# Attention forward and backward with a gated MLP on one core: ScalarE in program order, another order of loads at a hand-over, and a lag of seven row tiles

## The chip, the cores and the metric

The kernel runs on one core of one Trainium2 chip. The metric is the device time of one execution in microseconds (us). A ratio is the mean time of one kernel's fast runs over that of the other's of the same rounds, so it is not quite the ratio of the medians that are quoted. In the experiments the recorded ratios leave out the first, profiled run of each kernel, while the means that I quote in us keep it, so the two can differ by up to 2.5 us. In the profile lines PE is TensorE and PEld its weight loads, DVE is VectorE, ACT ScalarE, POOL GpSimd and SP SyncE; SPq is SyncE issuing transfers, and L958 is line 958 of the kernel. The granted clock is the share of TensorE's full clock that it was given, and the DMA share is the mean busy share of the 16 DMA engines.

## The reference

One layer, forward and backward. The layer is `out = x + attention(xn) * silu(mlp(xn))` with `xn = layernorm(x)`, 2048 rows of 576, 32 heads of 128 over a key and value cache of 2048, and a gated MLP of 4608. The outputs are `out` and the gradients of all inputs but one.

```python
def _A_ref(x, k_cache, v_cache, wq, wo):                 # H, Dh = 32, 128
    q = (x @ wq).reshape(B, Sq, H, Dh).transpose(0, 2, 1, 3)
    p = softmax(einsum("bhqd,bhkd->bhqk", q, k_cache) * Dh ** -0.5)
    o = einsum("bhqk,bhkd->bhqd", p, v_cache)
    return o.transpose(0, 2, 1, 3).reshape(B, Sq, H * Dh) @ wo
def _B_ref(x, w_gate, w_up, w_down):
    return (sigmoid(x @ w_gate) * (x @ w_up)) @ w_down
# ... x + s * g; reference() returns it and the vjp of grad_out
```

## The kernel before

Two stages matter here. In attention each head goes through 16 row tiles twice: first scores and exponentials, then their gradient. Each row tile leaves a slab of 128 x 2048 that a DMA transposes (PT in the first half, dST in the second), and a matmul group takes the transposed slab `SKEW` row tiles later. That distance is the lag, and one row tile's turn in a half is a slot.

```python
SKEW = 6
...
wpt = pool("wpt", 8 if fast else 4)          # transposed slabs in flight
...
def transpose_slab(hs, qt, name):
    T = wpt.tile([P, NT, P], bf, name=name, tag="PT")
    nc.sync.dma_start_transpose(T[:], hs.slabs[qt][:])
...
put(b1 + qt + skew, NT * P // 2, lambda qt=qt: tail1(hd(), qt, 0))   # reads PT
put(b2 + qt + skew, NT * P // 2, lambda qt=qt: tail2(hd(), qt, 0))   # reads dST
```

After attention comes the output projection: 16 row tiles, each a sum over 32 heads of the transposed attention output (oT) times rows of wo. Three oT buffers exist, which reuse the memory of KQ, xnT and xn_all, so in the profile tile 0's load is `KQ<-on_d`, tile 1's `xnT<-on_d`, tile 2's `xn_all<-on_d`. The last rows of wo are written over Kn, Vn and dOn, which attention frees last; heads whose rows lie there are "late", the others "early".

```python
loads[0] = row_loads(0)                       # dsg, g2b, xb of row tile 0
for st in range(1, R0):                       # R0 = 3
    if st > 1:
        nc.gpsimd.tensor_copy(oTs[st][0:1, 0, 0:1], loads[0][st % 3][0:1, 0:1])
    load_oT(oTs[st], st)
for view, h0, n, dead in wo_parts:
    if dead in (1, 2, 3):
        load_wo_rows(view, h0, 0, n)
for st in range(1, R0):
    loads[st] = row_loads(st)
...
def close(st):
    if st + R0 < NT:
        load_oT(oTs[st % 3], st + R0)
        loads[st + R0] = row_loads(st + R0)
    ...
for st in range(R0 - 1):
    mm(st, h_early)
for st in range(NT):
    mm(st, h_late if st in accs_of else h_early + h_late)
    close(st)
    if st == 0 and R0 > 1:
        mm(R0 - 1, h_early)
```

The copy of one element ahead of tile 2's load is not arithmetic: it reads what the first row loads bring and writes into the oT buffer, so it holds that load back until they have landed.

## Time and profile before

| | before |
|---|---|
| time | 4933.09 us, median of 3 (4931.61 to 4936.69) |
| TensorE busy, span | 4835.4 of 4929.9 us |
| one head of attention | 94.63 us, 32 heads |
| attention, projection, late stages | up to 3531.0, 143.4 and 1255.5 us |
| all waits of TensorE for transposed slabs | 13.1 us |
| waits in the hand-over to the projection | 6.8 us |

TensorE is the bound. The whole of its idle time is 4929.9 - 4835.4 = 94.5 us, of which the waits that the profile lists make up some 41; the rest lies before its first matmul and in gaps too short to list. The lines that carry this stand in the prediction.

### The profile page before, as it was taken

The page shows a single profiled execution, that of the slowest core. Times are in us where ns is not written, and L with a number is a line of the kernel's source. Part 1 is how long each engine was busy: PE and PEld are TensorE (multiplying, and loading weights), DVE is VectorE, ACT ScalarE, POOL GpSimd, SP SyncE. Part 2 cuts the span into 40 slices and gives each one's busy share as a digit, 9 for nine tenths or more (in the row PEclk, how much of TensorE's full clock was granted, in tenths as well). Part 3 has the DMA queues.
Part 4 walks back from the last instruction along what each step waited for, and adds up shares of the span by engine and source line. Part 5 has one row for each costly group of instructions (what it writes and reads, how often), then busy time and mean ns, then how long its engine had stood idle before and what let it go on. Part 6 is the DMA issues. An engine that isn't in the chain of part 4 may idle for free.

```text
span 4929.9 us, 100847 instructions
## 1 busy us (share of the span) xinstructions
PE 4835.4 (98%) x40273; PEld 2894.6 (59%) x41029; DVE 2802.5 (57%) x6554; ACT 2472.1 (50%) x4228; POOL 840.7 (17%) x1329
## 2 busy tenths in 40 slices
PE   9999999999999999999999999999899999999998
PEld 4445666666666666666666666666555555555554
DVE  4544666666666666656656666665434555554215
ACT  4431766766676676666667667667312111111111
POOL 3322111111111111111111111111221111111112
PEclk9999999999999999999999999999999999999999
DMA  7886999999999999999999999999999999998665
GB/s 260 274 201 170 225 227 231 215 227 230 227 232 224 230 227 227 233 221 233 223 224 228 232 226 223 232 229 224 225 221 234 230 232 225 226 224 213 187 173 153
DMA packets 3045845, 1097.11 MB, mean 223 GB/s; under 512 B 2949553, under 2 KB 2953778, under 8 KB 3045362
## 3 DMA queue, kind: packets, MB, share of 16 engines
q1 hardware_dynamic: 2946594, 771.07, 83.5%
q0 software_dynamic: 98160, 318.85, 20.5%
q8 instruction: 323, 5.29, 0.4%
q14 instruction: 160, 1.31, 0.1%
q10 hardware_dynamic: 608, 0.59, 0.0%
HBM read 175.31 MB, written 177.93 MB: 72 GB/s over the span
## 4 chain that ended last, share of the span: by engine, by line
PE 94%; DMA 2%; DVE 2%; issue 1%; ACT 1%; SPq 0%; POOL 0%; POOLq 0%; ACTq 0%; DVEq 0%
PE acc L683 18%; PE acc L744 18%; PE acc L998 13%; PE acc L1054 8%; PE dp L706 8%; PE sp L636 8%; PE acc L215 6%; PE u_ps L450 3%; PE dh L1111 3%; PE g_ps L448 3%; PE acc L533 3%; PE acc L958 2%; PE acct L145 1%; DMA dST<-Pq 1%; DVE Pq L709 1%
## 5 line engine op out<-in xcount | busy, mean ns | idle before, releaser
L654 ACT ACTIVATE Pq<-sp 128x1024 bf16<-128x1024 f32 x1024 | 1047.1, 1023 | 267.3 <-PE sp L636 224.3
L709 DVE SCALAR_TENSOR_TENSOR Pq<-dp,negdelta,Pq 128x1024 bf16<-128x1024 f32 x512 | 655.2, 1280 | 46.6 <-PE dp L706 45.2
L712 ACT ACTIVATE t<-dp,negdelta 128x1024 bf16<-128x1024 f32 x512 | 567.1, 1114 | 214.7 <-PE dp L706 165.3
L683 PEld LDWEIGHTS <-dST 128*128 128x128 bf16 x8192 | 508.2, 98 | 152.1 <-DMA dST<-Pq 11.0
L706 PE MATMUL dp<-VT,dOT 128*128 128x512 bf16 x1919 | 581.6, 379 | 2.4
L683 PEld LDWEIGHTS <-PT 128*128 128x128 bf16 x8192 | 500.1, 98 | 130.9 <-DMA PT<-Pq 11.1
L636 PE MATMUL sp<-KQ 128*128 128x512 bf16 x1858 | 568.9, 380 | 5.2 <-issue 5.2
L683 PE MATMUL acc<-Kn,dST 128*128 128x128 bf16 x8192 | 557.1, 219 | 8.8 <-DMA dST<-Pq 6.9
L683 PE MATMUL acc<-Vn,PT 128*128 128x128 bf16 x8192 | 542.1, 219 | 8.5 <-DMA PT<-Pq 6.2
L744 PE MATMUL acc<-Pq,dOn 128*128 128x512 bf16 x1983 | 527.3, 379 | 10.0
L713 DVE TENSOR_TENSOR Pq<-t,Pq 128x1024 bf16<-128x1024 bf16 x512 | 354.5, 692 | 316.7 <-ACT t L712 306.9
L744 PE MATMUL acc<-Pq,Qn 128*128 128x512 bf16 x2013 | 524.3, 380 | 4.9
L724 ACT ACTIVATE dq_n<-acc,rsc 128x128 bf16<-128x128 f32 x512 | 187.5, 366 | 333.7 <-PE acc L683 312.0
L1154 DVE TENSOR_TENSOR dxn<-acc,dxn 128x576 f32<-128x576 f32 x272 | 206.1, 758 | 247.8 <-PE acc L1054 247.8
L744 PEld LDWEIGHTS <-Qn 128*128 128x128 bf16 x2048 | 200.4, 98 | 240.9 <-issue 1.6
L744 PEld LDWEIGHTS <-dOn 128*128 128x128 bf16 x2048 | 198.8, 98 | 233.8
L1116 ACT ACTIVATE ndh<-dh 128x512 bf16<-128x512 f32 x144 | 86.0, 597 | 452.8 <-DVE du_blk L1114 449.0
L636 PEld LDWEIGHTS <-KQ 128*128 128x128 bf16 x2048 | 179.3, 98 | 127.7 <-issue 7.2
L641 DVE TENSOR_REDUCE rs_all<-rsp 128x1 f32<-128x2 f32 x512 | 78.5, 153 | 306.5 <-ACT Pq L654 295.0
L706 PEld LDWEIGHTS <-dOT 128*128 128x128 bf16 x2048 | 178.8, 98 | 124.4 <-issue 11.9
L677 POOL DMA_DIRECT2D on_d<-o_n x128 | 97.1, 759 | 778.8 <-DVE junk L695 447.8
L677 POOL DMA_DIRECT2D dq_d<-dq_n x128 | 97.9, 765 | 719.7 <-ACT dq_n L724 679.8
(208 smaller groups left out, 6794.4 us busy)
## 6 DMA issues: line engine op xcount, KB each, us to landing
out_dram<-kvn POOLq DMA_DIRECT2D x64, 512.0 KB, 4.7
ah<-a_d POOLq DMA_DIRECT2D x18, 1024.0 KB, 9.2
ah<-h_d POOLq DMA_DIRECT2D x18, 1024.0 KB, 12.1
h_d<-h_row POOLq DMA_DIRECT2D x64, 256.0 KB, 3.5
a_d<-a_row POOLq DMA_DIRECT2D x64, 256.0 KB, 3.8
x_all<-in_A_k_cache_dram SPq DMA_DIRECT2D x64, 256.0 KB, 3.8
on_d<-o_n POOLq DMA_DIRECT2D x128, 128.0 KB, 4.4
kvT_d<-KQ POOLq DMA_DIRECT2D x32, 512.0 KB, 5.3
```

What stands on the lines that cost most here:

```text
L215: nc.tensor.matmul(av[:, :CH], lhsT=w[:, i, :], rhs=srcT[:, i, cs], start=(i == 0), stop=(i == DT - 1))
L636: nc.tensor.matmul(sp[:, c * CH:(c + 1) * CH], lhsT=hs.QT[:, qt * P:(qt + 1) * P], rhs=hs.KT[:, hf * HW_ + c * CH: hf * HW_ + (c + 1) * CH ...
L654: nc.scalar.activation(Pq[:, hsl], sp[:], AF.Exp, scale=SCALE, accum_out=hs.rsp[:, hf:hf + 1])
L683: nc.tensor.matmul(hs.acc[:, 0, :], lhsT=T[:, kt, :], rhs=rhs[:, kt, :], start=(kt == 0), stop=(kt == NT - 1))
L706: nc.tensor.matmul(dp[:, c * CH:(c + 1) * CH], lhsT=hs.dOT[:, qt * P:(qt + 1) * P], rhs=hs.VT[:, hf * HW_ + c * CH: hf * HW_ + (c + 1) * C ...
L709: nc.vector.scalar_tensor_tensor(Pq[:, hsl], dp[:], hs.negdelta[:, qt:qt + 1], Pq[:, hsl], op0=ALU.add, op1=ALU.mult)
L712: nc.scalar.activation(t[:], dp[:], AF.Identity, bias=hs.negdelta[:, qt:qt + 1], scale=1.0)
L713: nc.vector.tensor_tensor(Pq[:, hsl], t[:], Pq[:, hsl], op=ALU.mult)
L744: nc.tensor.matmul(self.acc, lhsT=self.nat[:, qt, :], rhs=self.slabs[qt][:, cs], start=(qt == self.lo), stop=(qt == self.hi - 1))
L998: nc.tensor.matmul(acc[:, n0:n0 + nn], lhsT=lhs[:, st, cols], rhs=rhs[:, st, n0:n0 + nn], start=(st == 0), stop=(st == NT - 1))
L1054: nc.tensor.matmul(acc[:, n0:n0 + nn], lhsT=lT, rhs=w[:, n0:n0 + nn], start=(k == 0), stop=(k == len(terms) - 1))
L1154: nc.vector.tensor_tensor(dxn[:, st, :], acc[:, :D], dxn[:, st, :], op=ALU.add)
```

## The change

It has three parts. The lag goes from six to seven, with a ninth buffer for transposed slabs (paid for by smaller pools), so that a slab has one slot more to land. At the hand-over, wo's last rows are loaded ahead of the row loads, the rows that are freed last are loaded and summed last, and the holding copy is gone. In the late stages ScalarE keeps program order; before, a scheduler chose its order.

```diff
-    SKEW = 6
+    SKEW = 7
-            wpt = pool("wpt", 8 if fast else 4)
+            wpt = pool("wpt", 9 if fast else 4)
 ... (stat 8 -> 4 buffers, rs_all replaced by a small tile, junk in one buffer: room for the ninth slab)
-            tc.manual_schedule(engines={EngineType.SP, EngineType.Pool, EngineType.DVE, EngineType.PE}):
+            tc.manual_schedule():
-            h_late = [... for _, h0, n, dead in wo_parts if dead in (1, 2, 3) ...]
+            h_late = [... for _, h0, n, dead in sorted(wo_parts, key=lambda w: w[3] == 1) if dead in (1, 2, 3) ...]
-            loads[0] = row_loads(0)
             for st in range(1, R0):
-                if st > 1:
-                    nc.gpsimd.tensor_copy(oTs[st][0:1, 0, 0:1], loads[0][st % 3][0:1, 0:1])
                 load_oT(oTs[st], st)
-            for view, h0, n, dead in wo_parts:
+            for view, h0, n, dead in sorted(wo_parts, key=lambda w: w[3] == 1):
                 if dead in (1, 2, 3):
                     load_wo_rows(view, h0, 0, n)
+            loads[0] = row_loads(0)
```

More of the change, by code (lines that the diff above doesn't have):

```diff
@@ L598, in attention @@
             wsneg = None if fast else pool("wsneg", 3)
-            wpt = pool("wpt", 8 if fast else 4)
+            wpt = pool("wpt", 9 if fast else 4)
             wt, stg = pool("wt", 2), pool("stg", 2)
-            stat, hstat = pool("stat", 8), pool("hstat", 2)
+            stat, hstat = pool("stat", 4), pool("hstat", 2)
             ps_big = pool("ps_big", 2, space=PSUM)
@@ L610, in attention @@
             acc_box[0] = acc_alloc
-            warm = stat.tile([P, 1], f32, name="warm")
+            warm = stat.tile([P, 1], f32, name="rs")
             nc.scalar.activation(warm[:], eps_t[:], AF.Exp)
@@ L618, in start_head @@
                 hs = heads_pre[h] if h == 0 else new_head(h)
-                hs.rs_all = hstat.tile([P, NT], f32, name="rs_all")
                 hs.rinv_all = hstat.tile([P, NT], f32, name="rinv_all")
@@ L640, in row_sums @@
             def row_sums(hs, qt):
-                nc.vector.tensor_reduce(hs.rs_all[:, qt:qt + 1], hs.rsp[:], axis=AX.X, op=ALU.add)
-                nc.vector.reciprocal(hs.rinv_all[:, qt:qt + 1], hs.rs_all[:, qt:qt + 1])
+                rs = stat.tile([P, 1], f32, name="rs")
+                nc.vector.tensor_reduce(rs[:], hs.rsp[:], axis=AX.X, op=ALU.add)
+                nc.vector.reciprocal(hs.rinv_all[:, qt:qt + 1], rs[:])
                 hs.PT[qt] = transpose_slab(hs, qt, "PT")
@@ L693, in tail1 @@
                 alt.scaled(hs.o_n[:, qt % G4, :], op_[:, 0, :], hs.rinv_all[:, qt:qt + 1], eng=("s" if qt >= NT - skew else "v"))
-                junk = wt.tile([P, P], f32, name="junk")
+                junk = wt.tile([P, P], f32, name="junk", bufs=1)
                 nc.vector.scalar_tensor_tensor(junk[:], op_[:, 0, :], -1.0, hs.dOn[:, qt, :], op0=ALU.mult, op1=ALU.mult,
@@ L882 @@
     with late("pc") as pc, late("pcf") as pcf, \
-            tc.manual_schedule(engines={mybir.EngineType.SP, mybir.EngineType.Pool, mybir.EngineType.DVE, mybir.EngineType.PE}):
+            tc.manual_schedule():
         xn_all = pc.tile([P, NT, D], bf, name="xn_all")
@@ L925 @@
             h_early = [h0 + k for _, h0, n, dead in wo_parts if dead not in (1, 2, 3) for k in range(n)]
-            h_late = [h0 + k for _, h0, n, dead in wo_parts if dead in (1, 2, 3) for k in range(n)]
+            h_late = [h0 + k for _, h0, n, dead in sorted(wo_parts, key=lambda w: w[3] == 1) if dead in (1, 2, 3) for k in range(n)]
             oTs.append(oT_view(xn_all[:].rearrange("p t d -> p (t d)"), 0))
```

## The prediction

> **What bounds the kernel now.** I read the busy digits first, then the waits of TensorE by stretch, then the timeline where it waits. The busy view says that TensorE is the bound everywhere:
>
> ```profile
> PE   9999999999999999999999999999899999999998
> PEclk9999999999999999999999999999999999999999
> ...
> PE 94%; DMA 2%; DVE 2%; issue 1%; ACT 1%; SPq 0%; POOL 0%; POOLq 0%; ACTq 0%; DVEq 0%
> ```
>
> In the chain that ended last PE has 94%. A change of buffers and order can win only the rest, and only where PE stands still. So I looked at where it does. The waits of PE in attention (484 to 3535 us) and after it:
>
> ```profile
> PE acc L683 <- DMA dST<-Pq: 6.9, 6, 3.3
> PE acc L683 <- DMA PT<-Pq: 6.2, 5, 1.7
> PE sp L636 <- issue: 5.2, 2, 2.7
> ```
>
> ```profile
> PE acc L958 <- DMA Kn<-in_A_wo_dram: 2.8, 1, 2.8
> PE acc L958 <- DMA Vn<-in_A_wo_dram: 2.8, 1, 2.8
> PE acc L1054 <- DMA dqbT<-ah: 1.6, 1, 1.6
> PE acc L958 <- DMA xn_all<-on_d: 1.2, 1, 1.2
> ```
>
> (waiter, what ended the wait, us in total, times, longest.) The first two lines are the transposed slabs that come too late, all in all 11 waits in 1024 slabs. The second fence is the output projection, which waits for rows of wo (written over Kn and Vn) and for the third row tile's transposed attention output (in xn_all). The measured total is small: some 20 us of 4930.
>
> How regular attention is: every 64th weight load of line 636 starts a head. The distance is 94.63 us in 25 of the 31 gaps or within 0.01 of it; it is 98.78, 95.30, 95.25 and 96.26 after heads 5, 13, 22 and 23, and 89.61 in the first head, which has no head before it to finish. So a head without a wait costs 94.63, and the excess is 4.15 + 0.67 + 0.62 + 1.63 = **7.1 us**.
>
> The clock shows that a wait costs more than itself (window, PE, PEld, DVE, ACT, POOL busy, granted clock, DMA share, GB/s):
>
> ```profile
> 3440.00:3510.00 70.00, 66.28 (x605) 42.28 (x615) 49.22 (x134) 45.85 (x76) 13.52 (x26) 1.00 1.17 232
> 3510.00:3535.00 25.00, 21.46 (x184) 13.72 (x186) 7.24 (x10) 6.25 (x12) 2.41 (x4) 0.86 1.13 238
> 3535.00:3560.00 25.00, 17.97 (x112) 8.50 (x114) 2.98 (x4) 0.70 (x2) 10.78 (x20) 0.75 0.88 213
> 3560.00:3690.00 130.00, 127.95 (x1075) 71.22 (x1094) 44.54 (x76) 22.18 (x52) 33.05 (x60) 0.99 0.88 215
> ```
>
> The timeline of PE in the hand-over from attention to the projection:
>
> ```profile
> 3547.80 1.60 PE L958 MATMUL acc<-Kn,KQ 128*128 128x512 bf16 x6 [2.77 <-DMA Kn<-in_A_wo_dram]
> 3552.16 1.60 PE L958 MATMUL acc<-Vn,KQ 128*128 128x512 bf16 x6 [2.76 <-DMA Vn<-in_A_wo_dram]
> 3553.57 1.63 PE L958 MATMUL acc<-dOn,KQ 128*128 128x512 bf16 x6
> 3556.37 3.04 PE L958 MATMUL acc<-dsT,xn_all 128*128 128x512 bf16 x12 [1.16 <-DMA xn_all<-on_d]
> ...
> 3564.41 0.90 PE L958 MATMUL acc<-Kn,xnT 128*128 128x512 bf16 x6
> ```
>
> Six matmuls take 1.60 after the wait and 0.90 when the clock is back.
>
> **What the Trainium skill says.** "TensorE: Matmul & The Clock Gate", Part 1: The HAM clock gate: the array falls to half its clock after an idle window of about 3.4 us and needs about as long a busy one to return. The trace agrees: after the wait of 3.26 us at 3514.54 sixteen matmuls took 1.89 us, two slots earlier 1.06, and full pace is back at 3520.4. The same page, Architectural detail: ScalarE works its queue strictly in order. The trace agrees: a copy whose PSUM was complete at about 4914.8 ran at 4918.52, right behind an activation that waited for VectorE. So an order of ScalarE can matter. "DMA: Bandwidth & Descriptors", Issuing engines are not separate DMA queues: all queues share the same 16 engines. The trace agrees: the DMA share is 1.17 while slabs, wo rows and stores run together, and the transpose into xn_all, issued at 3540.43 beside three loads of wo rows, was awaited until 3556.37. The same page, Rules for kernel authors, says to issue early and wait late; that is what each part of this change does.
>
> **The change part by part.**
>
> *Lag seven, nine buffers.* No matmul is added or removed. The transposed slab of a row tile is now read one slot later. A slot is 94.63 / 32 = 2.96 us on average, so each slab has that much more time to land; the ninth buffer keeps the same spare (eight for six, nine for seven). The waits in heads 5, 13, 22 and 23 are 0.3 to 2.2 us long (weight loads included), below 2.96, so all should go: -7.1. Has ScalarE or VectorE room for the seventh tail in the other half of a head? In slots 5 and 6 of the score half PE needs 2.62 us. ScalarE starts one exp 1.14 after another there, and a dq copy adds 0.31: 2 x 1.14 + 0.31 = 2.59. It just fits, and the next slot has no dq copy. In the dp half VectorE had 0.52 idle in every second slot (5.24 us), with the tail's work in it. So I take 94.63 as unchanged. In the first head one tail of 16 x 55.8 ns = 0.89 moves into the second half and ramp slots 6 and 8 become about 0.2 longer: -0.7, including two short waits there.
>
> *The end of attention.* Here the lag helps little. The queue of transposes:
>
> ```profile
> 3481.24 23.32 SPq L630 DMA_TRANSPOSE dST<-Pq  x8
> 3504.67 4.80 SPq L584 DMA_TRANSPOSE KQ<-on_d  x1
> 3509.55 18.30 SPq L630 DMA_TRANSPOSE dST<-Pq  x8
> 3527.96 4.64 SPq L584 DMA_TRANSPOSE xnT<-on_d  x1
> ```
>
> It issues without a pause, some 10 us behind the slabs, because the last head also loads wo rows. The last dST landed at about 3530.2 and PE took it at 3530.54: at the end the transposes set the time, not the lag. Waits of PE before that (1.7, 0.4, 1.0, 3.3 and 3 of slow clock) turn into waits a little later. After the last slab PE has one slot's units instead of two: 6 matmuls of 0.215 us instead of 10, -0.9, and 0.2 nearer the landing: -1.1.
>
> *wo rows first, no copy that holds back xn_all.* The three loads of wo rows were issued at 3540.72, 5.9 us after the last kvT store (3534.85), behind three row loads and a GpSimd copy that waited for them. They now follow the store at once, Vn and dOn first and Kn, which is free last, last; the transpose into xn_all no longer waits for that copy (3540.22) and can go right after the one into xnT, at about 3532.7. Without any wait PE would go from the early heads of tile 1, which end at 3544.9, through the late heads of tile 0 (3 x 0.735 = 2.2) and the early ones of tile 2 (5.6) to 3552.7, where the trace has 3564.41: the whole hand-over is worth 11.7 at most. Will the loads land in time? kvT store 0.5 MB, wo rows 1.33 MB and xn_all 0.5 MB are 2.3 MB; the same stretch moved 3.65 MB in 18.7 us, 195 GB/s. That is 12 us from 3533.4, thus 3545.4, where PE wants the first rows at 3543.8 and the last at 3545.3. I leave 2 us of waits and 1.7 of slow clock: 11.7 - 3.7 = -8.0.
>
> *Program order on ScalarE.* The instruction order of the two kernels differs in the late stages by three places only: one ndh ahead of three copies in the first block, and two activations of the last rows ahead of a dwo copy. The two waits of PE on ndh are 0.8 us in all, and VectorE sets them. At the end a copy comes later and may hold a PSUM tile 0.9 us, but the last rows go at VectorE's pace of 4.36 us each and PE is not behind them. I take -0.2.
>
> Sum: -7.1 - 0.7 - 1.1 - 8.0 - 0.2 = **-17.1**, from 4933.1 to **4916.0 us**, 0.35% faster.
>
> **The rivals.** (1) *The lag shifts ScalarE or VectorE onto the path.* Slots 5 and 6 leave ScalarE 0.03 us; if slot 6 stalls PE by 0.3 in each of 31 heads, that is +9, and the result is 4925. For it: dp of the sixth slot came 0.06 us after VectorE had freed its PSUM. Against it: 25 heads equal to 0.01 us, so there is slack that doesn't show. (2) *The loads move the wait, not the end.* All share the DMA engines; if wo rows, the kvT store and xn_all together land no sooner than at 3550, the hand-over gives 4 instead of 9: 4920. For it: xn_all alone took almost 16 us. (3) *The waits in attention are chance*, other heads in each run (times range over 5 us); then one slot more takes them all, also those of slower runs, and the last slabs come sooner as well: 4908.
>
> **Range and chances.** The two big terms are 7.1 (certain to 3) and 9.1 (certain to 4); rival 1 can cost 9, rival 3 bring 8. I take 4906 to 4926. Two per cent are 98 us, and all that PE waits for anywhere, slow clock included, is below 60: faster by over 2% has 1%, within 2% has 98.5%, slower has 0.5%.
>
> **What would show it.** Right: heads of 94.63 with no excess after 5, 13, 22, 23; hardly a wait of line 683 in the middle of attention, but one of some 3 us still in the last slots; wo loads straight after the kvT store; the third tile begun some 10 us sooner after the last head's start; the last 100 us unchanged. Wrong: heads longer than 94.63 with waits of sp or dp for ScalarE or VectorE; a hand-over as long as before; no wait left at the end of attention.

Five slips in that text, none of which moves the result. 26 of the 31 gaps between heads are 94.63, not 25. The waits in the two fences add up to some 27 us, not 20. The sixteen matmuls that took 1.06 us stood one slot earlier, not two. TensorE's whole idle time, with the gaps too short to list, is 94.5 us, not below 60; it still stays below the 98 us that two per cent would need. And not each part of the change issues a transfer earlier: program order on ScalarE does not.

## The result, and the profile after

The changed kernel took 4933.99 us (median of 4, 4930.88 to 4944.1) against 4934.89 us of the kernel before in the same rounds: ratio 1.0002, 95% interval 0.9984 to 1.0019. The predicted 4916 us and the range of 4906 to 4926 were missed: the class, within two per cent, was right, but nothing of the 17 us came.

The profiled run was the slowest of the four (4944.1 us), so its waits are somewhat more than usual. The same lines of its page as shown of before, the busy digits and the chain that ended last:

```profile
PE   8999999999999999999999999999899999999998
...
PE 94%; DMA 2%; issue 2%; DVE 1%; SPq 1%; ACT 0%; POOL 0%; POOLq 0%; ACTq 0%; DVEq 0%
```

TensorE is as much the bound as before. The waits of TensorE in attention, and then after it (waiter, what ended the wait, us in total, times, longest):

```profile
PE acc L683 <- DMA PT<-Pq: 10.0, 10, 2.1
PE acc L683 <- DMA dST<-Pq: 8.2, 6, 2.8
```

```profile
PE acc L956 <- DMA KQ<-on_d: 9.6, 1, 9.6
PE acc L1052 <- ACT dqT L40: 6.4, 1, 6.4
...
PE acc L996 <- ACT dqT L40: 0.7, 1, 0.7
...
PE acc L956 <- DMA Kn<-in_A_wo_dram: 0.4, 1, 0.4
PE acc L956 <- DMA Vn<-in_A_wo_dram: 0.3, 1, 0.3
```

Three things are to be seen. The slabs are waited for longer than before (18.2 against 13.1 us), in spite of the larger lag. The waits for wo's rows are nearly gone (0.7 against 5.6 us), as intended. And a wait of 9.6 us has come that was not there: for tile 3's transposed output. The timeline of TensorE around it, and below it tile 3's line and its load in the kernel before, where there is no wait:

```profile
3549.01 0.90 PE L956 MATMUL acc<-Vn,KQ 128*128 128x512 bf16 x6 [0.25 <-DMA Vn<-in_A_wo_dram]
...
3552.04 4.33 PE L956 MATMUL acc<-dsT,xn_all 128*128 128x512 bf16 x34
...
3557.68 0.90 PE L956 MATMUL acc<-Vn,xnT 128*128 128x512 bf16 x6
...
3572.36 5.78 PE L956 MATMUL acc<-dsT,KQ 128*128 128x512 bf16 x34 [9.55 <-DMA KQ<-on_d]
```

```profile
3555.23 4.83 SPq L584 DMA_TRANSPOSE KQ<-on_d  x1
3569.38 4.33 PE L958 MATMUL acc<-dsT,KQ 128*128 128x512 bf16 x33
```

The projection's first matmul is at 3537.32 here, against 3533.59 before. Tile 1's late heads begin at 3557.68, thus 20.4 us after that; before it was 3564.41 - 3533.59 = 30.8. That gain of over 10 us is real, and it is given back at tile 3. The queue of transposing loads shows what tile 3 waited for:

```profile
3537.61 5.04 SPq L584 DMA_TRANSPOSE xn_all<-on_d  x1
3552.24 11.33 SPq L584 DMA_TRANSPOSE KQ<-on_d  x1
```

Tile 3's load can only be issued when tile 0 has released its buffer, at 3552.24. The issue took 11.33 us instead of some 5, and TensorE could start on the data at 3572.36. The stretches of that time (window, its length, busy time of PE, PEld, DVE, ACT and POOL, granted clock, DMA share, GB/s); the first two are the end of attention and the hand-over, the last three a closer look:

```profile
3510.00:3537.00 27.00, 21.09 (x213) 13.34 (x212) 7.74 (x9) 7.59 (x15) 1.61 (x3) 1.00 1.12 232
3537.00:3572.00 35.00, 25.05 (x205) 12.94 (x202) 8.61 (x13) 3.08 (x8) 11.78 (x21) 0.90 1.13 200
3549.50:3553.00 3.50, 2.99 (x24) 1.49 (x23) 0.05 (x1) 0.70 (x2) 2.27 (x5) 1.00 1.03 366
3557.00:3568.00 11.00, 5.81 (x54) 3.14 (x52) 4.82 (x8) 2.38 (x6) 0.06 (x1) 0.87 1.20 106
3571.50:3574.50 3.00, 2.14 (x9) 0.93 (x10) 0.00 (x0) 0.00 (x0) 2.13 (x4) 0.50 1.22 250
```

The last number of a line is the one to look at. While wo's rows and row loads alone are moved, 366 GB/s flow. While transposing loads alone are moved, it is 250, and 276 to 300 once the first half microsecond of that window is past. While both are in flight, from 3557 to 3568, it is 106, though the DMA engines count as busy all the time (share 1.20). So the row loads and tile 3's load, issued together, slow each other here. This is not a fixed rate of such a mix: in the kernel before, 2.06 MB of plain and 0.61 MB of transposing loads went at 268 GB/s together from 3546 to 3556 us, and the slabs, stores and wo rows at the end of attention at 232 from 3440 to 3510. Why this mix is so much slower is not known.

The wait of 6.4 us on dqT lies at 4582.74, where a transpose of dqT stood in the queue behind others. It appears in this profile only, of twenty, so I put it down to chance.

### The profile page after: what moved, and what is told of

Read it like the earlier page. It is cut to its first block, busy times and chain, and to the rows that moved or that the text cites. A ratio compares the mean times of both kernels' runs of the same rounds, so it can differ in the third digit from the quotient of the medians.

```text
span 4942.3 us, 101605 instructions
## 1 busy us (share of the span) xinstructions
PE 4871.7 (99%) x41029; PEld 2891.4 (59%) x41029; DVE 2789.9 (56%) x6522; ACT 2477.1 (50%) x4260; POOL 840.5 (17%) x1328
## 3 DMA queue, kind: packets, MB, share of 16 engines
q0 software_dynamic: 98160, 318.85, 20.8%
## 4 chain that ended last, share of the span: by engine, by line
PE 94%; DMA 2%; issue 2%; DVE 1%; SPq 1%; ACT 0%; POOL 0%; POOLq 0%; ACTq 0%; DVEq 0%
PE acc L683 18%; PE acc L744 17%; PE acc L996 13%; PE sp L635 9%; PE dp L706 8%; PE acc L1052 8%; PE acc L215 6%; PE u_ps L450 3%; PE g_ps L448 3%; PE dh L1109 3%; PE acc L533 3%; PE acc L956 2%; PE acct L145 1%; DVE Pq L709 1%; DMA PT<-Pq 1%
## 5 line engine op out<-in xcount | busy, mean ns | idle before, releaser
L635 PE MATMUL sp<-KQ 128*128 128x512 bf16 x2048 | 609.8, 380 | 5.4 <-issue 5.4
L706 PE MATMUL dp<-VT,dOT 128*128 128x512 bf16 x2048 | 608.8, 379 | 2.2
L641 DVE TENSOR_REDUCE rs<-rsp 128x1 f32<-128x2 f32 x512 | 78.7, 154 | 369.1 <-ACT Pq L654 362.1
```

The lines of the kernel that those rows point to most:

```text
L635: nc.tensor.matmul(sp[:, c * CH:(c + 1) * CH], lhsT=hs.QT[:, qt * P:(qt + 1) * P], rhs=hs.KT[:, hf * HW_ + c * CH: hf * HW_ + (c + 1) * CH ...
L706: nc.tensor.matmul(dp[:, c * CH:(c + 1) * CH], lhsT=hs.dOT[:, qt * P:(qt + 1) * P], rhs=hs.VT[:, hf * HW_ + c * CH: hf * HW_ + (c + 1) * C ...
```

## The experiments

Eighteen runs were made, some of them of the same kernel, in five groups; a group ran on one chip with its own runs of the kernel before. Stage lengths below are measured alike in each trace: the first head is the distance of the first score weight loads of heads 0 and 1; the excess is the sum over heads 1 to 30 of what their length exceeds 94.62 us; the projection runs from its first weight load to its last; the late stages from there to the end. One thing has to be allowed for: the first weight load comes 2.58 us ahead of the projection's first matmul with a lag of six and 1.94 us with seven. So the projection of a kernel with a lag of seven looks 0.6 us shorter in these figures than it is beside one with six.

### Group 1: the change again, and its two large parts alone

The changed kernel, unaltered: 

> The changed kernel once more, unaltered. Theory A (a new wait took the place of the one removed): the profile again has a wait of PE on tile 3's transposed attention output (KQ<-on_d) at the hand-over, of 5 to 12 us, on every run, because that load can be issued only when tile 0 closes and now meets the row loads and has 7 us less time; the time stays within 0.2% of before. Theory B (a chance slow spell of the transposing loads in the one profile, at 800 to 1040 us and again at 3555 to 3572 us): the wait on KQ<-on_d is below 2 us here, the heads' waits sit in other heads or are gone, and the time falls towards 4920. The waits inside attention (10.3 us of excess in heads 4 and 5 of the first profile) should move to other heads under both theories; if they stay in heads 4 and 5 they are the change's own. The wait of 6.4 us on dqT in the last stage: if chance, it is gone or elsewhere here.

Median 4935.79 us of 5 (4927.23 to 4947.14), ratio 0.9995 (0.9982 to 1.0008). The wait on tile 3's load is there again, 9.65 us, and the projection took 147.5 us. So theory A holds for that wait. The excess in the heads, 17.9 us, sits once more in heads 3 to 5 (14 of it) but also in 19, 21 and 23. The wait of 6.4 us on dqT is gone.

The kernel before, for a second profile: 

> The kernel before, unaltered, only for a second profile. If the slow spells of the transposing loads are chance, the heads whose length exceeds 94.63 us are others than heads 5, 13, 22 and 23, with a total excess of 3 to 12 us; if they belong to the schedule, the same heads show them. The hand-over's gap (tile 1's late heads at 3564.41 in the first profile, some 143 us after head 31 begins) should be within 2 us of that in any case, since it is tied to the order of the loads.

One run, 4933.86 us. The excess is 5.1 us and lies in heads 4, 21, 24, 26 and 27, where the first profile had 5, 13, 22 and 23. Slow spells of the transposing loads thus fall elsewhere in each execution. Tile 1's late heads began 30.95 us after the projection did, against 30.82 in the first profile; counted from the start of head 31, as my expectation had it, they are 4.5 us later, since the end of attention itself varies.

The lag alone: 

> The kernel before with the lag of seven, the ninth buffer and the buffer cuts that pay for it, and nothing else of the change. My recorded sum gives this part -7.1 (waits inside attention) -0.7 (first head) -1.1 (end) = -9 us, so 4924 to 4926. The rival, that attention's waits are slow spells longer than the slack that one more slot of 2.96 us buys, gives -1 to -3 us, a ratio of 0.9995 or nearer to 1. Steady heads stay at 94.6 us under both. If ratio is above 1.0005, the lag costs something that neither names.

```diff
-    SKEW = 6
+    SKEW = 7        # with wpt 9, stat 4, rs in its own tile, junk in one buffer
```

Median 4927.16 us of 5 (4923.37 to 4938.07), ratio 0.9991 (0.9978 to 1.0004). The excess is 1.5 us, in one head, and the first head takes 88.2 us. On the mean it is 6.3 us faster than before: between the two expectations.

The reordered loads alone: 

> The kernel before with the reordering of the loads at the hand-over alone (wo's last rows ahead of the row loads, the last-freed rows summed last, no GpSimd copy ahead of tile 2's transposed load). My recorded term: -8 us (4925). Theory A above: tile 1's late heads begin 6 to 8 us earlier, but tile 3 begins no earlier than before, 148 to 150 us after head 31 begins, with a wait of 5 to 10 us on KQ<-on_d; the ratio is within 0.0005 of 1. Theory B: no such wait, ratio 0.998 to 0.9988.

```diff
 (the hand-over's part of the diff above, on the kernel before)
```

Median 4931.41 us of 6 (4923.08 to 4949.34), ratio 1.0001 (0.9985 to 1.0016). Here the projection took 136.8 us, 6.7 less than before, since the wait for tile 3 is only 3.2 us:

```profile
3559.78 3.83 PE L956 MATMUL acc<-dsT,KQ 128*128 128x512 bf16 x20 [3.22 <-DMA KQ<-on_d]
```

That is neither A nor B. It raised the question why the whole change has 9.6 us there, and led to theory C: the lag of seven makes it worse.

### Group 2: do the parts collide, and can the wait be taken away?

Lag and loads together, ScalarE as before: 

> The changed kernel with ScalarE's late order given back to the scheduler: lag seven and the reordered hand-over together. Theory C (the two parts collide: with the lag of seven the last transposes of attention and the projection's transposed loads are issued some 1.1 us later against the hand-over than in the run with the reordered hand-over alone, wo's rows take 10 to 12 us instead of 7 to 8, the row loads are pushed back, and tile 3's transposed load, issued then, takes 20 us instead of 14): the wait on KQ<-on_d is 8 to 11 us again, and the projection (first to last of its weight loads) takes 143 to 148 us. Theory D (ScalarE's order is what delays it): the wait is 3 us or less and the projection takes 136 to 138 us, as with the reordered hand-over alone. The wait of 0.7 us on dqT at line 996, seen in both profiles of the full change and in no other, should be gone in either case. Time within 0.1% of before under C, 0.998 under D.

```diff
-            tc.manual_schedule():
+            tc.manual_schedule(engines={EngineType.SP, EngineType.Pool, EngineType.DVE, EngineType.PE}):
```

Median 4931.64 us of 6 (4923.92 to 4945.54), ratio 0.9988 (0.9971 to 1.0006). The wait on tile 3 is 9.62 us and the projection 143.8: theory C, and not ScalarE's order. The time, 0.12% under before, lies between what C and D gave. The wait of 0.7 us on dqT is gone, as both expected.

A fourth oT buffer: 

> The changed kernel with a fourth buffer for the transposed attention output (in a slab that is free by then), so that tile 3's load is issued with those of tiles 1 and 2, ahead of the hand-over's row loads, and each later load when the tile that had its buffer closes. If tile 3's wait comes from its late issue, after tile 0's close: the wait on KQ<-on_d is gone (below 1 us) and the projection takes 133 to 137 us, 8 to 11 us less than in the full change; ratio 0.997 to 0.9985. Rival: the DMA engines are simply full in these 40 us, so the wait moves to wo's rows, to xn_all or to the tile after, and the projection still takes over 140 us.

```diff
+            oTs.append(oT_view(ah0[:].rearrange("p a t f -> p (a t f)"), 0))
+            oT_of = [0, 1, 2, 3] * 3 + [0, 1, 2, 0]
-            for st in range(1, R0):
+            for st in range(1, 4):
                 load_oT(oTs[st], st)
```

Median 4930.38 us of 6 (4921.15 to 4948.78), ratio 0.9985 (0.9965 to 1.0004). Tile 3 waits 2.1 us, tile 4 waits 3.2, wo's rows 0.8, and the projection takes 138.0 us: in part the first expectation, in part the rival. The wait moved, at over half its size.

Fewer row loads in flight: 

> The changed kernel with fewer row loads in flight at the hand-over: tile 1's rows are loaded when tile 0 closes, tiles 2 and 3's when tile 1 closes, and each later tile's two tiles ahead. Three oT buffers as before. If it is the row loads that slow tile 3's transposed load: it lands 12 to 15 us after its issue instead of 20, and the wait is 2 to 5 us; projection 136 to 140 us. If it is only the late issue, the landing still takes 18 to 20 us and the wait stays at 8 to 10 us. A loss is possible where a tile's rows come late for VectorE and hold back ScalarE's copies; it would show as waits of PE on s_sb at the projection.

```diff
             loads[0] = row_loads(0)
-            for st in range(1, R0):
-                loads[st] = row_loads(st)
 ...            (in close, after tile st's output is stored:)
+                for nx in ((1,) if st == 0 else (2, 3) if st == 1 else (st + 2,)):
+                    loads[nx] = row_loads(nx)
```

Median 4943.66 us of 6 (4927.6 to 4956.18), ratio 1.0009 (0.9989 to 1.0029). Tile 3 starts without any wait, 10.4 us after its load was issued at 3543.88, where the full change needs 20. So it is the row loads beside it that make this load slow. But the projection took 160.5 us, worse than I had allowed for: wo's rows were waited for 5.3 us, later tiles' loads 2.9 and 1.3, VectorE's late rows 2.3, and the last tile's load fell together with 2 MB that the next stage loads. The lines of that run, TensorE at tile 3 and the queue of transposes at the last tile:

```profile
3554.28 4.33 PE L954 MATMUL acc<-dsT,KQ 128*128 128x512 bf16 x33
```

```profile
3645.41 14.54 SPq L584 DMA_TRANSPOSE KQ<-on_d  x1
```

An issue of 14.54 us, and a wait of 9.5 us behind it: it looks like the same collision at another place. Why holding the rows brings these waits I did not follow up.

Program order alone: 

> The kernel before with program order on ScalarE in the late stages alone. My recorded term is -0.2 us. From the two profiles of the full change: one wait of 0.6 us on ndh goes, one of 0.7 us on dqT comes, so the late stages (end of the projection to end of the kernel) take 1255.0 to 1256.1 us, as in the kernel before (1255.5 and 1255.0). The 6.4 us wait on dqT of one of the two profiles was a late transpose: no such wait here.

```diff
-            tc.manual_schedule(engines={EngineType.SP, EngineType.Pool, EngineType.DVE, EngineType.PE}):
+            tc.manual_schedule():
```

One run, 4940.3 us, beside a mean of 4939.9 of the kernel before. The late stages took 1255.3 us, as expected; the wait of 0.7 us on dqT came, but the two on ndh stayed (0.8 us in all), so that it is the reordered loads that take one of them away.

### Group 3: repetition, the other direction, and the waits taken apart

Fourth buffer with held row loads: 

> The changed kernel with the fourth oT buffer of the run before, and the row loads of tiles 1 and 2 held until tile 0 closes, those of tiles 3 and 4 until tile 1 closes; from then on three ahead as ever. If late issue and contention with the row loads share tile 3's wait (the fourth buffer alone left 2.1 us on tile 3 and 3.2 us on tile 4; holding the rows alone made tile 3's load land in time), both waits are gone: projection 132 to 135 us and a ratio of 0.997 to 0.9985. Rival: wo's three row loads, which landed 9 to 17 us after issue in the runs so far, now end last, and the wait sits on them: projection 136 to 140 us.

```diff
 (the fourth buffer, and in close:)
-                    loads[st + R0] = row_loads(st + R0)
+                    if st > 1:
+                        loads[st + R0] = row_loads(st + R0)
 ...            (after tile st's output is stored:)
+                for nx in ((1, 2), (3, 4))[st] if st < 2 else ():
+                    loads[nx] = row_loads(nx)
```

Median 4929.72 us of 5 (4921.72 to 4933.6), ratio 0.9986 (0.9973 to 0.9999). Neither tile 3 nor tile 4 waits. In their place wo's first late rows are waited for 5.4 us, and the projection takes 138.4: the rival.

The reordered loads alone again: 

> The reordered hand-over alone once more, since its short projection (136.75 us, a wait of 3.2 us on tile 3) rests on one profile. Theory C (the lag of seven is what turns 3.2 into 9.6): 135 to 139 us and a wait of 2 to 5 us again. Rival (chance decides in each execution): a wait of over 8 us, projection 143 us or more.

Median 4937.8 us of 6 (4925.03 to 4940.94), ratio 1.0002 (0.9990 to 1.0013). Tile 3 waits 6.0 us, the projection takes 140.0. Just over my bounds, between the two readings: shorter than before, with a wait that varies.

A lag of five: 

> The kernel before with a lag of five row tiles instead of six, eight buffers as before: one step the other way. If the wait inside attention is a matter of slack, as my prediction's first term has it, one slot (2.96 us) less turns every place with under 3 us of slack in the trace of before into a wait: the heads' excess over 94.62 us rises from 5 to 11 us (four profiles at lag six) to 20 to 40, and the time by 0.3 to 0.7%. If a lag of one slot hardly matters, because the transposing queue is over 90% occupied and its backlogs outlast a slot, the excess stays at 5 to 14 us and the time within 0.2%. The first head, 89.6 to 90.1 us at lag six and 87.2 to 89.0 at seven, should take 91 to 92 us in either case.

```diff
-    SKEW = 6
+    SKEW = 5
```

Median 4959.13 us of 5 (4948.64 to 4962.24), ratio 1.0040 (1.0028 to 1.0053). The excess is 29.0 us and the first head takes 94.1. The waits of TensorE from head 1 to 30:

```profile
PE acc L683 <- DMA PT<-Pq: 15.6, 18, 2.1
PE acc L683 <- DMA dST<-Pq: 9.1, 13, 2.0
```

31 waits, where the kernel before has 6 in the same heads of its first profile. So slack is what counts; only the first head was worse than I had said.

The lag of seven alone again: 

> The lag of seven alone once more. Its first run stood at 0.9991 with an interval that holds 1, and its profile had 1.5 us of excess in the heads, against 0.1 to 17.9 in the five other profiles with a lag of seven. If the lag is worth my recorded -9 us, the ratio is 0.998 to 0.9985 and the excess again under 3 us; if it is worth only the first head's -1.8 us, the ratio is 0.9993 to 1.0 and the excess anything from 0 to 18. The projection takes 142 to 144 us with no wait on KQ<-on_d in either case.

Median 4932.03 us of 5 (4926.1 to 4935.91), ratio 0.9994 (0.9981 to 1.0006), excess 1.6 us, projection 143.2. The excess is as the first expectation had it, the ratio as the second.

### Group 4: why the whole shows less than its parts

The changed kernel a third time: 

> The changed kernel a third time. Summed from its parts alone (lag: -6.3 and -4.1 us on the mean of the runs; hand-over: -2.1 and -0.1; program order: none) it should gain some 5 us, but nine runs of it have shown +0.3. Theory E (chance: heads 4 to 6 fell into slow spells in both profiles): the mean of these five runs is 4 to 7 us under before, the excess in the heads 0 to 10 us. Theory F (something in the whole costs 5 us): the mean is within 2 us of before. The wait on KQ<-on_d of tile 3 is 8 to 11 us in both.

Median 4932.77 us of 6 (4927.23 to 4942.98), ratio 0.9995 (0.9977 to 1.0012); on the mean 1.7 us under before. Wait on tile 3: 10.3 us. Excess 8.8 us. This meets F, just, and not E, which wanted 4 us; with a spread of 16 us among the six runs the two can hardly be told apart.

Lag and loads again: 

> Lag seven and the reordered hand-over, ScalarE's late order left to the scheduler, once more (-6.9 us on the mean in its first rounds). Under E it stands where the full change stands in these rounds, within 3 us; under F, with the program order as the cost, it is 5 to 8 us faster than the full change, and its late stages are shorter by that much, which no profile so far shows. Wait on tile 3's load 8 to 11 us, projection 142 to 146 us.

Median 4930.3 us of 6 (4923.02 to 4937.94), ratio 0.9991 (0.9974 to 1.0007), 4.9 us under before and some 3 under the full change of the same rounds: between E and F. The late stages take 1255.3 us, no shorter. A miss in one point: tile 3 waited only 0.7 us, and the projection took 138.9. In this execution wo's rows came so late that they, not tile 3, were waited for:

```profile
3549.54 1.60 PE L956 MATMUL acc<-Vn,KQ 128*128 128x512 bf16 x6 [4.40 <-DMA Vn<-in_A_wo_dram]
...
3565.64 4.34 PE L956 MATMUL acc<-dsT,KQ 128*128 128x512 bf16 x33 [0.74 <-DMA KQ<-on_d]
```

When tile 3's load was issued, all but one of the twelve row loads of tiles 0 to 3 had been issued, and the last of them landed 3.9 us later; in the third run of the full change all but three, tile 3's own, and the last landed 18 us later. Tile 3's load was through within 12 us, there it took 20.8. It is the collision again, seen from its absence: where the two kinds of load overlap for only 3.9 us, the wait is nearly gone.

Program order alone, timed: 

> Program order on ScalarE alone, now timed. Under E: the mean within 2 us of before, late stages 1255 to 1256 us with one wait of 0.7 us on dqT more and one of 0.6 us on ndh fewer. Under F with the program order as the cost: 4 to 8 us slower than before.

Median 4940.2 us of 6 (4931.88 to 4949.55), ratio 1.0007 (0.9989 to 1.0025), on the mean 4.6 us slower. Late stages 1255.7 us, with the wait of 0.7 us on dqT. Excess 17.9 us. The time fits F, the late stages fit E.

Loads kept apart in time: 

> The changed kernel with a fourth oT buffer as before, but tile 3's transposed load held back until the last of wo's rows has landed (by a copy of one element that reads the one and writes the other), and the row loads of tiles 1 and 2 held until tile 0 closes. If the wait at the hand-over is contention between transposed loads and wo's rows in one direction and between row loads and transposed loads in the other, keeping the three apart takes both away: wo's rows land 9 to 12 us after the hand-over begins with a wait under 1 us, tile 3's load lands before 27 us, and the projection takes 132 to 135 us (143.5 before); ratio about 0.998. If wo's rows still land at 14 to 17 us, it was not tile 3's load that slowed them in the last run, and the projection takes 137 to 140 us.

```diff
+            nc.gpsimd.tensor_copy(oTs[3][0:1, 0, 0:1], wo_of[h_late[-1]][0:1, 0:1])
+            load_oT(oTs[3], 3)         # after loads[0] = row_loads(0); rows 1 to 4 held as above
```

Median 4932.15 us of 6 (4922.16 to 4938.47), ratio 0.9990 (0.9972 to 1.0007). Tile 3 doesn't wait, but wo's first late rows still land 15.8 us after the projection begins (a wait of 4.4), VectorE's late rows cost another 2.6, and the projection takes 142.3, more than either expectation. So it was not tile 3's load that slowed wo's rows in the run with the fourth buffer and held rows. What remains beside them is tile 2's transposing load, into xn_all, and the kvT store ahead of them.

That can be read across the runs with the reordered loads. wo's first late rows were always issued 2.08 us after the projection began. How late they landed goes, between groups, with when the load into xn_all was issued (both in us from the projection's first matmul):

| run | lag | xn_all issued | first late wo rows landed |
|---|---|---|---|
| loads alone, two runs | six | -1.28, -0.87 | 9.7, 9.0 |
| lag and loads; with fourth buffer | seven | -0.35, -0.48 | 10.7, 11.2 |
| full change, three runs | seven | 0.29, 0.31, 0.38 | 11.6, 14.3, 14.7 |
| lag and loads, second run | seven | 0.31 | 15.8 |
| held rows; fourth and held; timed; fourth and held without program order | seven | 0.22, 0.22, 0.21, 0.30 | 16.7, 16.8, 15.8, 15.6 |

In the last three lines the load is issued at nearly the same time and the rows land anywhere from 11.6 to 16.8, so the issue time is not the whole of it. With the holding copy in place, as in the kernel before, that load is issued at 6.8 to 7.0 whatever the lag, and the late rows at 7.1 and later. The copy did one thing that I had not seen: the kvT store, issued 1.25 us after the first matmul in every run, lands at 4.2 to 5.3 us in the eight profiles with the copy and at 7.7 to 12.0 in the twelve without it. No run keeps the copy and moves wo's rows alone.

### Group 5: a test of the pattern, and the version that is best

Program order alone, a third time: 

> Program order on ScalarE alone, a third time, as a test of a pattern seen only afterwards: the nine profiles with program order had 10.5 us of excess in the heads on average (0.1 to 17.9), the eight without it at lag six or seven 5.6 (1.5 to 12.0), though the instruction order in attention is the same. Chance: the mean of these runs within 3 us of before, excess anywhere from 2 to 12. A real cost of the whole program, by a way that I can't name: 4 to 6 us slower than before, excess 8 or more.

Median 4937.36 us of 6 (4924.91 to 4948.73), ratio 1.0003 (0.9988 to 1.0019), on the mean 2.7 us slower; excess 9.8 us. The time meets "chance", near its limit of 3 us, the excess both. The wait that program order brings, in this run:

```profile
PE acc L998 <- ACT dqT L40: 0.7, 1, 0.7
```

It is in all ten profiles with program order and in none without.

Fourth buffer, held rows and lag seven, ScalarE left to the scheduler: 

> The fourth oT buffer with held row loads and the lag of seven (0.9986 in its first rounds), with ScalarE's late order left to the scheduler: the candidate to beat both kernels. Chance: 0.9980 to 0.9992, as with program order. A real cost of program order: 0.9970 to 0.9980. The hand-over as in the run with program order: no wait on tile 3 or 4 above 1 us, one of 4 to 6 us on wo's first late rows, projection 137 to 139 us.

Median 4923.53 us of 6 (4921.27 to 4935.65), ratio 0.9981 (0.9968 to 0.9993), on the mean 9.1 us faster than before in the same rounds. The interval lies below 1, so this version beats the kernel before by some 0.2%, and its median lies 9 us or more under the changed kernel's of any group. It is the best of several tried, though, and has one set of rounds. The ratio meets "chance", at its edge. Its hand-over:

```profile
3545.57 1.60 PE L957 MATMUL acc<-Vn,KQ 128*128 128x512 bf16 x6 [4.21 <-DMA Vn<-in_A_wo_dram]
...
3559.80 4.33 PE L957 MATMUL acc<-dsT,ah 128*128 128x512 bf16 x33
```

Tile 3 (now in ah) starts without a wait, one wait of 4.2 us on wo's rows is left, and the projection takes 136.9 us.

### The stages side by side

| kernel | first head | excess, heads 1 to 30 | projection | late stages |
|---|---|---|---|---|
| before, 2 profiles | 89.6, 89.7 | 7.3, 5.1 | 143.4, 143.5 | 1255.5, 1255.0 |
| changed, 3 | 88.0, 89.0, 88.4 | 10.3, 17.9, 8.8 | 143.5, 147.5, 148.2 | 1263.5, 1255.6, 1255.7 |
| lag alone, 2 | 88.2, 88.8 | 1.5, 1.6 | 142.5, 143.2 | 1255.6, 1255.7 |
| loads alone, 2 | 89.7, 90.2 | 4.9, 12.0 | 136.8, 140.0 | 1255.1, 1255.7 |
| lag and loads, 2 | 87.6, 87.9 | 4.1, 8.3 | 143.8, 138.9 | 1255.1, 1255.3 |
| program order alone, 3 | 90.1, 90.1, 89.6 | 10.7, 17.9, 9.8 | 146.4, 144.0, 143.1 | 1255.3, 1255.7, 1255.6 |
| lag five, 1 | 94.1 | 29.0 | 145.5 | 1255.9 |

The times, as means less the mean of the kernel before in the same rounds:

| kernel | runs | us against before |
|---|---|---|
| lag alone | 5, 5 | -6.3, -4.1 |
| loads alone | 6, 6 | -2.1, -0.1 |
| program order alone | 6, 6 | +4.6, +2.7 |
| lag and loads | 6, 6 | -6.9, -4.9 |
| changed | 4, 5, 6 | +0.8, 0.0, -1.7 |

A least-squares fit of these 62 runs (the single one of program order included) and the 59 of the kernel before, with one level per group of rounds and one term per part, gives lag -4.7, loads -0.6 and program order +4.3 us, each with a standard error of 1.5. This is an estimate from those runs. Together that is -1.0; the runs of the changed kernel average -0.5. Without the first, profiled run of each kernel in the experiments the same fit gives -4.6, -0.1 and +2.8, with standard errors of 1.7.

## Why the prediction was wrong, step by step

**TensorE is the bound; only its waits can be won.** Right, in every profile. It is why the class was right.

**Lag seven leaves a head at 94.63.** Right: undisturbed heads take 94.61 to 94.62 us in the changed kernel, so rival 1 is out; ScalarE and VectorE had the room.

**"So all should go: -7.1".** This step failed. The mechanism, slack against late slabs, was right, and the lag of five shows it: one slot less costs 20 us of excess. But I took the four waits of one profile for a fixed list. The second profile of before has them in other heads, and slow spells come in all sizes: single waits of up to 4.3 us stand in profiles with a lag of seven, longer than the 2.96 us that one slot buys. The mean excess is 9.7 us in seven profiles with a lag of six and 7.4 in twelve with a lag of seven, thus -2.3 instead of -7.1; like with like it is -2.8 without program order (7.3 and 4.5) and -3.4 with it (12.8 and 9.4). A saturated queue is one reason that fits, and was not tested: in heads 1 to 30 of the kernel before the transposing loads occupy their queue for 92% of the time, so a backlog drains slowly and outlasts a slot. The gain from five to six was large and that from six to seven small. No run separates the lag of seven from the ninth buffer and the smaller pools that pay for it.

**First head -0.7.** Right in kind and too small: 88.1 against 89.9 us on the mean, thus -1.8.

**End of attention -1.1.** The step "0.9 less after the last slab" did happen: the last slab lands 2.24 to 2.27 us before the projection's first matmul with seven and 3.10 or more with six, wherever the trace has the landing. From the start of the last head to that matmul it takes 113.6 us with a lag of six and 112.9 with seven, on the mean. That fits the term, but single profiles scatter by 2 us, so the whole is not resolved.

**Hand-over "11.7 - 3.7 = -8.0".** This step failed most. The first half of it was right: wo's rows were issued right behind the kvT store, and in the first profile they were waited for 0.7 us (some 3 us in the two later ones). What I left out was everything after tile 2. With three oT buffers tile 3's load is not issued before tile 0 closes, so making tile 0 to 2 earlier makes tile 3 late; and it then runs beside row loads, at 106 GB/s for both together, and is waited for 9.6 to 10.3 us in the three profiles of the changed kernel. My check of whether the loads land in time used a mean rate of 195 GB/s, and a mean hides that the rate depends on what flows together. With a lag of six the part gives 3.4 and 6.7 us in the projection of two profiles, though the timed runs of that kernel are only 0.1 and 2.1 us faster, within the noise. With a lag of seven it gives nothing in the full change: 143.5, 147.5 and 148.2 against 142.5 and 143.2 of the lag alone. Part of why is in the end of attention: the 0.9 us that the lag saves there brings the projection nearer to its own loads. The load into xn_all is then issued after the first matmul instead of before it, wo's rows land later, and the row loads and tile 3 follow, one behind another. The issue times and the landing times show this order. That xn_all makes the rows late is argued from the table above, and so is that no third cause takes part. The first run of lag and loads (xn_all at -0.35, and still 9.6 us of wait) shows that the wait for tile 3 is not set by xn_all alone. Rival 2, that the loads move the wait and not the end, was right in its title, and I let it leave 4 us of the gain where it took all. Its mechanism, that wo's rows and xn_all land too late, was not what happened in the first profile, so this was in part luck.

**Program order -0.2.** The step saw the right place and chose the wrong side: "may hold a PSUM tile 0.9 us" is the wait of 0.7 us on dqT, present in all ten profiles with program order. That accounts for about half a microsecond of the late stages. The fit's +4.3 us (+2.8 without the profiled runs) is more, and the rest of it is not found. The ten profiles with program order have 10.4 us of excess in the heads on average and the nine without it, lag five apart, 5.8, although the order of instructions in attention is the same in both. The two further runs made to test this, at +2.7 us and a ratio of 0.9981, both met what chance would give, close to its limit. So whether program order costs 4 us, and how it could, stays open; chance is not excluded.

In sum, -17.1 was made of -8.9 for the lag, -8.0 for the loads and -0.2 for the order, and the runs give about -4.7, -0.6 and +4.3.

The skill's pages named in the prediction held where they were used, with one reserve. "TensorE: Matmul & The Clock Gate", Part 1: The HAM clock gate, says that the clock drops after an idle window of about 3.4 us; after the wait of 9.55 us the granted clock of 3571.5 to 3574.5 is 0.50, so that a long wait costs more than itself, while a group after a wait of 0.25 us took the usual 0.90 us. The sizes agree less well than I wrote: in the kernel before a wait of only 2.77 us was enough (granted clock 1.00 from 3545.1 to 3547.6, 0.50 from 3547.8 to 3549.4), and after the wait of 3.26 us full pace came back 5.9 us after work did. "DMA: Bandwidth & Descriptors", Rules for kernel authors, asks to issue early; tile 3's load is the one that this change could not issue early (3552.24, behind tile 0).

## What to carry to other kernels

Before a load is moved ahead, list what the stage needs after it, with the buffer that each later load must wait for: a gain at tile 1 is worth nothing if tile 3 is bound to the release of tile 0. Estimate the time of a load from the rate of just those transfers together, not from a stage's mean: the rate here ran from 106 to 366 GB/s. And where waits come from slow spells, take several profiles before adding up the waits of one: here the excess of one and the same changed kernel ran from 8.8 to 17.9 us in three profiles, a spread larger than the 7.1 us that I hoped to gain there.

## What the Trainium skill lacked or had wrong

- No page that I read gives the rate of transposing and plain loads in flight together. "DMA: Bandwidth & Descriptors", Queues, rings and completion order, says that the engines take turns between queues, which would lead one to expect a rate between those of the two. In the changed kernel's hand-over it was 366 GB/s for plain loads alone, 276 to 300 for transposing loads alone and 106 for both, with the engines busy; in the kernel before both together reached 268. The cause is not known.
- "Advanced Engine Details and Errata", X-Bar Transpose (TRN2), says that transposing DMAs are as fast as plain ones. Here 276 to 300 against 366 GB/s in the same run; "DMA: Bandwidth & Descriptors", Latency and other measured facts, has 261 GB/s for one form of transposing load, which is nearer to this.
- No page that I read gives the spread in time between executions of a whole program: 59 runs of the kernel before lie between 4923 and 4948 us at a granted clock of 0.996 to 0.998, and the excess of the heads in its two profiles fell on different heads.
